# Turning v by VectorE in 32x32 blocks instead of by TensorE

## The chip, the core and the metric

The kernel runs on one core of a Trainium2 chip. The metric is the device time of one execution in microseconds (us), the median of several runs. The core's engines each work through a queue of their own in order: TensorE (PE in the profile; its weight loads are PEld), VectorE (DVE), ScalarE (ACT), GpSimd (POOL) and SyncE (SP), which here only issues DMAs. They wait for each other by semaphores. 16 DMA engines move data between device memory (HBM) and on-chip memory (SBUF); TensorE writes to PSUM, eight banks of 128 x 512 float32.

## The reference

Channel attention, and then a gated convolution over its output, for B = 4 batches of N = 6336 rows and C = 256 channels:

```python
qn = q / (np.linalg.norm(q, axis=1, keepdims=True) + 1e-06)
kn = k / (np.linalg.norm(k, axis=1, keepdims=True) + 1e-06)
s = kn.transpose(0, 2, 1) @ qn / tau
a = softmax(s)                                # 256 x 256 for each batch
x = v @ a
gate_pre[t] = sum(conv_w[j] * x[t - 4 + j] for j in range(5))   # x is 0 before row 0
gate = 1 / (1 + exp(-gate_pre))
out = (gate * (x @ w_val)) @ w_out
```

All inputs and the output are float32.

## The kernel before

**Two kinds of work.** A batch's scores s are summed in PSUM (s_ps) over 17 groups of rows of q and k; three rows per partition make a group (tile raw). A batch's output is made in 13 chunks of up to 508 rows of v, each with 4 rows of halo, so there are 52 steps (b, i). Batch 0's 17 groups come first, alone. From then on the remaining groups are spread over the steps up to the 36th ("steps with scores", until about 500 us); the last 16 steps have none ("steps without scores").

**Precision.** Most products are made of rounded parts: an operand is cast to a hi half (by ScalarE) and the rest is its lo half (one subtraction), and three products hi·hi, hi·lo, lo·hi are summed. So v has tiles v_hi and v_lo, the gated values g_hi and g_lo, and the scores' raw gets hi.

**A step.** `product` needs v with channels on partitions and rows along the free dimension, but v lies in memory by rows. `load_v` brings a chunk to v_raw by one DMA issued from SP (128 rows by 1 KB pieces, 512 KB). `transpose_v` turns it on TensorE, four 128x128 transposes for each half of the channels, to PSUM (t_ps, L359); ScalarE casts that to v_hi (L360) and VectorE subtracts to v_lo (L361). `conv` makes x_ps = v @ a by 6 products for each half h (L369); ScalarE scales the first tap to gate (L383) and VectorE adds the other four (L385). `sigmoid` (L391) is one instruction for both halves. `value` makes val_ps by 6 products with a @ w_val (L369), and VectorE multiplies it into gate (L398). `split_g` makes g_hi on ScalarE (L411) and g_lo on GpSimd (L412). `finish` makes 24 products with w_out (o_ps, L428), ScalarE copies them (L438) and issues the two stores (L443, L445).

**A group of scores.** ScalarE casts hi (L196) and squares (sq, L213), GpSimd makes the lo half (L197); VectorE and GpSimd add up the squares for the norms (L218); TensorE makes the products (L232). `softmax` of a batch is a chain of small instructions cut into pieces, which `tick` places between other work.

**What sets the order.** The program is written as a software pipeline: step n makes sigmoid(n), conv(n+1), value(n), split_g(n), transpose_v(n+2) and finish(n-1), and asks for load_v(n+3). A scheduler then orders each engine's queue by its own model of time, within what the program holds fast (`behind`, `high_priority`). Buffers tie queues together: three of v_raw, three of v_hi and v_lo, two banks of x_ps, and four banks shared by t_ps, val_ps and o_ps. A DMA also waits for the eighth DMA before it, whichever of SP and ScalarE issued that, since eight semaphores go round.

Of the kernel before, what the change touches and what calls it, by code (L numbers as in the profile page):

```python
# [29 lines left out]
def kernel(  # L30
# [301 lines left out]
    vraw, vt = {}, {}  # L332

    def load_v(b, i):

# [2 lines left out]
        j0 = 0
        if i == 0:
            nc.gpsimd.memset(t[0:HALO, 0, :], 0.0)  # L340
            nc.sync.dma_start(out=t[HALO:P, 0, :], in_=v[b, 0:P - HALO])
            j0 = 1
        full, rest = divmod(HALO + w, P)
        lo = t0 - HALO
        nc.sync.dma_start(out=t[:, j0:full, :], in_=v[b, lo + j0 * P:lo + full * P].rearrange("(j p) c -> p j c", p=P))
        if rest:
            nc.sync.dma_start(out=t[0:rest, full, :], in_=v[b, lo + full * P:t0 + w])
        vraw[b, i] = t

    def transpose_v(b, i, h):  # L350
        w = HALO + chunks[i][1]
        if h == 0:
            vt[b, i] = [v_p.tile([P, NH, HALO + WMAX], F32R, name=name) for name in ("v_hi", "v_lo")]
        th, tl = vt[b, i]
        src = vraw[b, i]
        tp = ps.tile([P, 512], F32, name="t_ps", tag="bank")
        for j in range(-(-w // P)):
            np_ = min(P, w - j * P)
            marks["PE"] = nc.tensor.transpose(tp[:, j * P:j * P + np_], src[0:np_, j, h * P:(h + 1) * P], ident[0:np_, 0:np_])  # L359
        nc.scalar.copy(th[:, h, 0:w], tp[:, 0:w])  # L360
        nc.vector.tensor_tensor(tl[:, h, 0:w], tp[:, 0:w], th[:, h, 0:w].bitcast(F32), ALU.subtract)  # L361
# [14 lines left out]
    def conv(b, i, h):  # L376
# [7 lines left out]
        for tap in range(1, K):  # L384
            nc.vector.scalar_tensor_tensor(gate[:, h, 0:w], x_ps[:, tap:tap + w], cw[:, h, tap:tap + 1],  # L385
                                           gate[:, h, 0:w], ALU.mult, ALU.add)

# [249 lines left out]
```

## Time and profile before

| | |
|---|---|
| median of 3 runs | 655.57 us (655.3 to 656.13) |
| profiled execution: span, first to last instruction | 653.5 us |
| granted TensorE clock, mean | 0.998 |
| read from HBM, written | 79.11 MB, 25.95 MB |

The profile is of one execution, whose span is 2.1 us (0.3%) under the median; the median also holds what lies around the instructions. An engine is busy while one of its instructions runs; issuing a DMA and waiting are not counted as busy. "x_ps<-v_hi,w" is an instruction that writes x_ps and reads v_hi and w. In a line of a group stand its count, its busy us in all, the mean ns of one, and after the last bar how long the engine had stood idle before these instructions and what ended that. Matmuls overlap, so their own lengths are longer than the distance from one to the next. The chain is the work that ended last, followed back from the last instruction through what released it.

### The profile page before, as it was taken

Reading aid. Unit: us, or ns where it says so; the run is one execution under the profiler, and the core shown is the slowest. Engines: PE = TensorE matmul, PEld = TensorE weight load, DVE = VectorE, ACT = ScalarE, POOL = GpSimd, SP = SyncE. Lnnn points to the kernel's source line nnn. Section 1 sums busy time; section 2 is a strip of 40 time slices with the busy share of each in tenths; the row PEclk is TensorE's granted clock in tenths of the full one; section 3 lists DMA queues with packets and bytes.
Section 4 is the critical chain, followed back from the end, with each engine's and each line's share of the span. In section 5 each row is a group of like instructions: output and inputs, shape, how many; then the busy total and the mean of one; then the engine's idle time right before and its main releaser. Section 6 shows DMA issues by size and latency. Waiting matters only on the chain.

```text
span 653.5 us, 10735 instructions
## 1 busy us (share of the span) xinstructions
PE 638.5 (98%) x4040; PEld 572.4 (88%) x4040; DVE 509.2 (78%) x831; ACT 466.8 (71%) x612; POOL 372.7 (57%) x181
## 2 busy tenths in 40 slices
PE   8899899999999999999999999999999899999996
PEld 7788699999989999998998999999989798888886
DVE  3694788887858787777877788887777879888884
ACT  4466978768688886777679887686877755655564
POOL 2591787949645786767855489496763122212221
PEclk9999999999999999999999999999999999999999
DMA  8999864646545564555645366453322343343213
GB/s 259 331 329 346 265 211 144 196 135 193 151 135 163 182 206 136 187 162 156 190 143 159 122 220 192 158 181 96 88 63 87 99 123 106 110 130 106 63 48 104
DMA packets 107876, 105.77 MB, mean 162 GB/s; under 512 B 5744, under 2 KB 107312, under 8 KB 107824
## 3 DMA queue, kind: packets, MB, share of 16 engines
q1 hardware_dynamic: 82048, 79.76, 39.6%
q10 hardware_dynamic: 25776, 25.32, 12.3%
q8 instruction: 32, 0.52, 0.3%
q14 instruction: 20, 0.16, 0.1%
HBM read 79.11 MB, written 25.95 MB: 161 GB/s over the span
## 4 chain that ended last, share of the span: by engine, by line
PE 87%; ACT 5%; SPq 3%; POOL 2%; issue 1%; DMA 1%; DVE 0%; ACTq 0%
PE o_ps L428 21%; PE x_ps L369 20%; PE val_ps L369 19%; PE s_ps L232 19%; PE t_ps L359 6%; SPq L75 2%; POOL hi L197 2%; DMA raw<-in_k_dram 1%; PE o_ps L318 1%; ACT hi L196 1%; ACT sq L213 1%; ACT L391 1%; ACT s L292 0%; SPq L125 0%; SPq L120 0%
## 5 line engine op out<-in xcount | busy, mean ns | idle before, releaser
L385 DVE SCALAR_TENSOR_TENSOR gate<-x_ps,wa,gate 128x508 f32<-128x508 f32 (+1 forms) x416 | 273.9, 716 | 15.8 <-ACT gate L383 14.9
L197 POOL TENSOR_TENSOR hi<-raw,hi 128x1536 fp32r<-128x1536 f32 (+2 forms) x51 | 166.1, 3259 | 103.2 <-ACT hi L196 103.2
L412 POOL TENSOR_TENSOR g_lo<-gate,g_hi 128x1016 fp32r<-128x1016 f32 (+1 forms) x50 | 117.5, 2351 | 125.9 <-ACT g_hi L411 125.8
L218 DVE TENSOR_TENSOR acc_ps<-acc_ps,sq 128x512 f32<-128x512 f32 (+1 forms) x124 | 86.5, 698 | 81.2 <-ACT sq L213 79.3
L369 PE MATMUL x_ps<-v_hi,w 128*128 128x512 f32 (+1 forms) x416 | 138.6, 392 | 0.5 <-DVE gate L385 0.3
L369 PE MATMUL val_ps<-v_hi,w 128*128 128x508 f32 (+1 forms) x416 | 134.1, 382 | 0.6 <-DVE w L323 0.5
L232 PE MATMUL s_ps<-hi 128*128 128x256 f32 (+1 forms) x846 | 119.6, 286 | 2.8 <-POOL hi L197 2.8
L232 PEld LDWEIGHTS s_ps<-hi 128*128 128x128 f32 (+1 forms) x846 | 109.6, 190 | 7.1 <-POOL hi L197 3.6
L428 PE MATMUL o_ps<-wo_hi,g_hi 128*128 128x256 f32 x400 | 112.9, 282 | 1.4 <-ACT at L313 1.4
L438 ACT COPY o_sb<-o_ps 128x512 f32<-128x512 f32 x99 | 58.2, 590 | 76.8 <-PE o_ps L428 76.6
L428 PE MATMUL o_ps<-wo_lo,g_hi 128*128 128x256 f32 x400 | 112.3, 281 | 0.0
L428 PE MATMUL o_ps<-wo_hi,g_lo 128*128 128x256 f32 x400 | 112.0, 280 | 0.0
L218 POOL TENSOR_TENSOR acc<-acc,sq 128x512 f32<-128x512 f32 x68 | 88.1, 1296 | 36.8 <-ACT sq L213 35.7
L213 ACT ACTIVATE sq<-raw 128x1536 f32<-128x1536 f32 (+3 forms) x69 | 95.9, 1393 | 15.8 <-DMA raw<-in_k_dram 10.4
L369 PEld LDWEIGHTS x_ps<-v_hi,w 128*128 128x128 f32 x416 | 77.4, 188 | 16.1 <-DVE gate L385 1.7
L369 PEld LDWEIGHTS val_ps<-v_hi,w 128*128 128x128 f32 x416 | 77.1, 188 | 14.4 <-DVE w L323 1.0
L383 ACT ACTIVATE gate<-x_ps,wa 128x508 f32<-128x508 f32 (+1 forms) x104 | 68.1, 669 | 18.8 <-PE x_ps L369 18.1
L398 DVE TENSOR_TENSOR gate<-val_ps,gate 128x508 f32<-128x508 f32 (+1 forms) x104 | 64.3, 657 | 21.7 <-ACT gate L391 20.0
L369 PE MATMUL x_ps<-v_lo,w 128*128 128x512 f32 (+1 forms) x208 | 79.6, 383 | 0.0
L369 PE MATMUL val_ps<-v_lo,w 128*128 128x508 f32 (+1 forms) x208 | 79.0, 380 | 0.0
L360 ACT CAST v_hi<-t_ps 128x512 fp32r<-128x512 f32 (+1 forms) x104 | 55.5, 570 | 32.9 <-PE t_ps L359 32.9
L428 PEld LDWEIGHTS o_ps<-wo_hi,g_hi 128*128 128x128 f32 x400 | 75.3, 188 | 2.3 <-ACT at L313 1.6
(80 smaller groups left out, 800.3 us busy)
## 6 DMA issues: line engine op xcount, KB each, us to landing
raw<-in_q_dram SPq DMA_DIRECT2D x64, 384.0 KB
raw<-in_k_dram SPq DMA_DIRECT2D x64, 384.0 KB
v_raw<-in_v_dram SPq DMA_DIRECT2D x44, 512.0 KB
out_dram<-o_sb ACTq DMA_DIRECT2D x47, 384.0 KB
out_dram<-o_sb ACTq DMA_DIRECT2D x47, 124.0 KB
v_raw<-in_v_dram SPq DMA_DIRECT2D x4, 384.0 KB
raw<-in_q_dram SPq DMA_DIRECT2D x4, 128.0 KB
raw<-in_k_dram SPq DMA_DIRECT2D x4, 128.0 KB
```

The costliest lines, as they stand in the source:

```text
L197: nc.gpsimd.tensor_tensor(hi[r, js, :, 1, :], raw[r, js, :, :], hi[r, js, :, 0, :].bitcast(F32), ALU.subtract)
L213: nc.scalar.activation(sq[0:np_, ja:jb], raw[0:np_, ja:jb], AF.Square)
L218: add = eng.tensor_tensor(st[key][0:np_], st[key][0:np_], sq[0:np_, j], ALU.add)
L232: marks["PE"] = nc.tensor.matmul(st["s"][:, h, :], lhs, rhs, start=False, stop=stop and h == NH - 1 and n_ == len(ops) - 1)
L360: nc.scalar.copy(th[:, h, 0:w], tp[:, 0:w])
L369: marks["PRODUCT"] = nc.tensor.matmul(ps, wt[:, which, ws, ch, hs], vs[:, ch, lo:hi_], start=n_ == 0, stop=n_ == 3 * NH - 1)
L383: nc.scalar.activation(gate[:, h, 0:w], x_ps[:, 0:w], AF.Copy, scale=cw[:, h, 0:1])
L385: nc.vector.scalar_tensor_tensor(gate[:, h, 0:w], x_ps[:, tap:tap + w], cw[:, h, tap:tap + 1], gate[:, h, 0:w], ALU.mult, ALU.add)
L398: nc.vector.tensor_tensor(gate[:, h, 0:w], val_ps[:, 0:w], gate[:, h, 0:w], ALU.mult)
L412: nc.gpsimd.tensor_tensor(gl[:, :, 0:w], gate[:, :, 0:w], gh[:, :, 0:w].bitcast(F32), ALU.subtract)
L428: nc.tensor.matmul(o_ps[:, u * C:(u + 1) * C], gs[:, h, off:off + P], ws[:, h, :], start=n_ == 0, stop=n_ == 3 * NH - 1)
L438: marks["ACT"] = nc.scalar.copy(o_sb[:, j:j + len(pair), :], o_ps[:, 0:len(pair) * C].rearrange("p (j c) -> p j c", c=C))
```

## The change

v is brought so that each 32x32 block lands in the quarter of the partitions where it belongs: v_raw now has dimensions [channel block j and row r in the block, half, block g of 32 rows, 32 channels], with eight DMAs for a chunk (four j, two h; sixteen for a batch's first chunk), each of 32 partitions and pieces of 128 bytes. Two VectorE instructions for each chunk (one for each half) then transpose all 32x32 blocks in place. ScalarE casts both halves in one instruction from SBUF. The lo halves are subtracted from SBUF: half 0 on VectorE and half 1 on GpSimd while groups of scores are left, both in one GpSimd instruction afterwards. Once all groups have been issued, the last of the five taps is no longer VectorE's: ScalarE scales it into a tile part, and GpSimd adds part to gate (all but the very last step). TensorE's transposes of v, and t_ps, are gone.

```diff
+    VW = -(-(HALO + WMAX) // Q) * Q                  # Q = 32
+    def span_v(i):
+        t0, w = chunks[i]
+        cols = -(-(HALO + w) // Q) * Q
+        base = min(t0 - HALO, N - cols)
+        return base, cols, t0 - HALO - base
     def load_v(b, i):
-        t = raw_p.tile([P, NT, C], F32, name="v_raw", bufs=3)
...
-        nc.sync.dma_start(out=t[:, j0:full, :], in_=v[b, lo + j0 * P:lo + full * P].rearrange("(j p) c -> p j c", p=P))
+        t = raw_p.tile([P, NH, VW // Q, Q], F32, name="v_raw", bufs=3)
+        for j in range(P // Q):
+            part = t[j * Q:(j + 1) * Q]
+            if base < 0:
+                nc.gpsimd.memset(part[0:-base, :, 0, :], 0.0)
+            for h in range(NH):
+                c0 = h * P + j * Q
...
+                nc.sync.dma_start(out=part[:, h, g0:g, :],
+                                  in_=v[b, base + g0 * Q:base + cols, c0:c0 + Q].rearrange("(g r) q -> r g q", r=Q))
-    def transpose_v(b, i, h):
...
-            marks["PE"] = nc.tensor.transpose(tp[:, j * P:j * P + np_], src[0:np_, j, h * P:(h + 1) * P], ident[0:np_, 0:np_])
-        nc.scalar.copy(th[:, h, 0:w], tp[:, 0:w])
-        nc.vector.tensor_tensor(tl[:, h, 0:w], tp[:, 0:w], th[:, h, 0:w].bitcast(F32), ALU.subtract)
+    def transpose_v(b, i):
...
+        for h in range(NH):
+            nc.vector.transpose(t[:, h, 0:g, :], t[:, h, 0:g, :])
+        marks["V"] = nc.scalar.copy(th[:, :, 0:g, :], t[:, :, 0:g, :])
+        for hs, eng in ((slice(0, 1), nc.vector), (slice(1, NH), nc.gpsimd)) if issued < len(all_groups) else ((slice(0, NH), nc.gpsimd),):
+            eng.tensor_tensor(tl[:, hs, 0:g, :], t[:, hs, 0:g, :], th[:, hs, 0:g, :].bitcast(F32), ALU.subtract)
     def conv(b, i, h):
...
-        for tap in range(1, K):
+        by_two = K - 1 if issued == len(all_groups) and all_steps.index((b, i)) < len(all_steps) - 1 else K
+        for tap in range(1, by_two):
             nc.vector.scalar_tensor_tensor(gate[:, h, 0:w], x_ps[:, tap:tap + w], cw[:, h, tap:tap + 1],
                                            gate[:, h, 0:w], ALU.mult, ALU.add)
+        for tap in range(by_two, K):
+            part = split_p.tile([P, WMAX], F32, name="part", tag="sq", bufs=2)[:, 0:w]
+            nc.scalar.activation(part, x_ps[:, tap:tap + w], AF.Copy, scale=cw[:, h, tap:tap + 1])
+            nc.gpsimd.tensor_tensor(gate[:, h, 0:w], gate[:, h, 0:w], part, ALU.add)
```

The scheduler orders the queues anew. Three places matter for what follows. The numbers behind names are buffers; in brackets stands what a row waits for (PE_, DVE_, Activation_, Pool_ are the engines, DMAHW0_ to DMAHW7_ the eight DMA semaphores).

SP in a step with scores, about the middle of the program, before: one load of v and the loads of q and k around it.

```order
L345 DMA v_raw_4119<-in_v_dram 128x4x256 [waits DMAHW5_49,PE_49]
L75 DMA raw_4139<-in_q_dram 128x3x256 [waits DMAHW6_49,Activation_49,Pool_49]
L75 DMA raw_4139<-in_k_dram 128x3x256 [waits DMAHW7_49]
L345 DMA v_raw_4258<-in_v_dram 128x4x256 [waits DMAHW3_49,DMAHW2_49,PE_49]
L75 DMA raw_4214<-in_q_dram 128x3x256 [waits DMAHW3_49,Activation_49,Pool_49]
L75 DMA raw_4214<-in_k_dram 128x3x256 [waits DMAHW4_49]
```

The same place after, where the gaps in the DMA numbers (1 and 3) are ScalarE's two stores:

```order
L76 DMA raw_4133<-in_k_dram 128x3x256 [waits DMAHW4_49]
L358 DMA v_raw_4243<-in_v_dram 32x16x32 [waits DMAHW5_49,DVE_49,Pool_49]
L358 DMA v_raw_4243<-in_v_dram 32x16x32 [waits DMAHW6_49]
L358 DMA v_raw_4243<-in_v_dram 32x16x32 [waits DMAHW7_49]
L358 DMA v_raw_4243<-in_v_dram 32x16x32 [waits DMAHW0_49]
L358 DMA v_raw_4243<-in_v_dram 32x16x32 [waits DMAHW2_49]
L358 DMA v_raw_4243<-in_v_dram 32x16x32 [waits DMAHW4_49]
L358 DMA v_raw_4243<-in_v_dram 32x16x32 [waits DMAHW5_49]
L358 DMA v_raw_4243<-in_v_dram 32x16x32 [waits DMAHW6_49]
L76 DMA raw_4208<-in_q_dram 128x3x256 [waits DMAHW7_49,Activation_49,Pool_49]
```

One row waiting for TensorE has become eight, the first of which waits for VectorE and GpSimd, and a store between them waits for the DMA eight before it, here a load of v or of q and k.

VectorE in the same step before, at the end of one chunk's work and the start of the next (gate_3901 and gate_4027 are the two chunks' gates):

```order
L218 TENSOR_TENSOR acc_ps_3575<-acc_ps_3575,sq_4019 128x512 [waits Activation_49]
L398 TENSOR_TENSOR gate_3901<-val_ps_4052,gate_3901 128x240 [waits PE_49,Activation_49]
L398 TENSOR_TENSOR gate_3901<-val_ps_4060,gate_3901 128x240 [waits DVE_49,PE_49]
L218 TENSOR_TENSOR acc_ps_3575<-acc_ps_3575,sq_4019 128x512 [waits DVE_49]
L361 TENSOR_TENSOR v_lo_4073<-t_ps_4074,v_hi_4072 128x512 [waits Activation_49]
L361 TENSOR_TENSOR v_lo_4073<-t_ps_4081,v_hi_4072 128x512 [waits Activation_49]
L385 SCALAR_TENSOR_TENSOR gate_4027<-x_ps_4028,wa_109,gate_4027 128x508 [waits Activation_49]
```

And after:

```order
L219 TENSOR_TENSOR acc_ps_3563<-acc_ps_3563,sq_4015 128x512 [waits Activation_49]
L414 TENSOR_TENSOR gate_3899<-val_ps_4048,gate_3899 128x240 [waits PE_49,Activation_49]
L414 TENSOR_TENSOR gate_3899<-val_ps_4056,gate_3899 128x240 [waits DVE_49,PE_49]
L219 TENSOR_TENSOR acc_ps_3563<-acc_ps_3563,sq_4015 128x512 [waits DVE_49]
L367 STREAM_TRANSPOSE v_raw_4243<-v_raw_4243 128x512 [waits DMAHW5_49,DMAHW7_49,DMAHW2_49,Pool_49]
L370 TENSOR_TENSOR v_lo_4220<-v_raw_3984,v_hi_4219 128x512 [waits Activation_49]
L367 STREAM_TRANSPOSE v_raw_4243<-v_raw_4243 128x512 [waits DMAHW6_49,DMAHW4_49,DMAHW0_49]
L397 SCALAR_TENSOR_TENSOR gate_4023<-x_ps_4024,wa_109,gate_4023 128x508 [waits Activation_49]
```

Two lo halves have become one lo half and two transposes, the transposes of a chunk a step ahead of its lo half and ahead of the next chunk's taps. The lo half v_lo_4069, whose v_raw buffer is the one that v_raw_4243 is loaded into, stands 15 rows above the first of these transposes; between them are two L414, eight taps and two sums.

ScalarE at batch 0's softmax before (s to exp, row sums to z, then a; `acc` and `sq` belong to batch 1's first groups):

```order
L209 ACTIVATE acc_455<-raw_356 128x512 [waits DMAHW7_49,DMAHW0_49]
L213 ACTIVATE sq_490<-raw_356 128x512 [waits Activation_49]
L292 ACTIVATE s_432,o_ps_465<-s_432,m_485 128x256 [waits DVE_49,PE_49]
L292 ACTIVATE s_432,o_ps_465<-s_432,m_485 128x256 [waits Activation_49]
L299 ACTIVATE a_507<-s_432,rz_505 128x256 [waits DVE_49]
```

And after:

```order
L210 ACTIVATE acc_477<-raw_373 128x512 [waits DMAHW6_49,DMAHW5_49]
L214 ACTIVATE sq_512<-raw_373 128x512 [waits Activation_49]
L368 CAST v_hi_603<-v_raw_379 128x1024 [waits DMAHW4_49,DMAHW3_49,DMAHW5_49,DMAHW2_49,DMAHW6_49,DMAHW1_49,DMAHW7_49,DMAHW0_49,DVE_49]
L293 ACTIVATE s_463,o_ps_487<-s_463,m_507 128x256 [waits DVE_49,PE_49]
L293 ACTIVATE s_463,o_ps_487<-s_463,m_507 128x256 [waits Activation_49]
L368 CAST v_hi_734<-v_raw_388 128x1024 [waits DMAHW4_49,DMAHW3_49,DMAHW5_49,DMAHW2_49,DMAHW6_49,DMAHW1_49,DMAHW7_49,DMAHW0_49,DVE_49]
L300 ACTIVATE a_529<-s_463,rz_527 128x256 [waits DVE_49]
```

The casts of the second and third chunk of v have come up into the softmax, ahead of the exponentials and of a, and wait for those chunks' loads and transposes.

More of the change, by code (lines that the diff above doesn't have):

```diff
@@ L23 @@
 VLEAD = 2
+Q = 32
 SIDE, LAST = 5, 15
@@ L332 @@
     vraw, vt = {}, {}
-    def load_v(b, i):
-        t0, w = chunks[i]
-        t = raw_p.tile([P, NT, C], F32, name="v_raw", bufs=3)
[L338 to L347, printed above, removed]
-        vraw[b, i] = t
@@ L350, in transpose_v @@
-    def transpose_v(b, i, h):
[L351 to L361, printed above, removed]
+    VW = -(-(HALO + WMAX) // Q) * Q
@@ new lines, in span_v @@
+    def span_v(i):
[3 more added lines that the diff above has]
+        return base, cols, t0 - HALO - base
+    def load_v(b, i):
+        base, cols, _ = span_v(i)
+        g = cols // Q
+        t = raw_p.tile([P, NH, VW // Q, Q], F32, name="v_raw", bufs=3)
[5 more added lines that the diff above has]
+                c0 = h * P + j * Q
+                g0 = 0
+                if base < 0:
+                    nc.sync.dma_start(out=part[-base:Q, h, 0, :], in_=v[b, 0:Q + base, c0:c0 + Q])
+                    g0 = 1
+                nc.sync.dma_start(out=part[:, h, g0:g, :],
+                                  in_=v[b, base + g0 * Q:base + cols, c0:c0 + Q].rearrange("(g r) q -> r g q", r=Q))
+        vraw[b, i] = t
@@ new lines, in transpose_v @@
+    def transpose_v(b, i):
+        g = span_v(i)[1] // Q
+        th, tl = vt[b, i] = [v_p.tile([P, NH, VW // Q, Q], F32R, name=name) for name in ("v_hi", "v_lo")]
+        t = vraw.pop((b, i))
+        for h in range(NH):
[3 more added lines that the diff above has]
+            eng.tensor_tensor(tl[:, hs, 0:g, :], t[:, hs, 0:g, :], th[:, hs, 0:g, :].bitcast(F32), ALU.subtract)
@@ L363, in product @@
     def product(ps, wt, which, b, i, h, lo, hi_):
-        th, tl = vt[b, i]
+        th, tl = (t.rearrange("p h g q -> p h (g q)") for t in vt[b, i])
+        at = span_v(i)[2]
+        lo, hi_ = at + lo, at + hi_
         hs = slice(h * P, (h + 1) * P)
@@ L525 @@
     tick()
-    with tc.high_priority(), behind("PE", "ACT"):
-        for h in range(NH):
-            transpose_v(*step(0), h)
+    with tc.high_priority(), behind("ACT"):
+        transpose_v(*step(0))
     with behind("PE", "ACT"):
@@ L550 @@
             nc.scalar.copy(wo_hi.rearrange("p h e -> p (h e)"), w_raw["out"][:, :, 1].bitcast(F32))
-    for h in range(NH):
-        transpose_v(*step(1), h)
+    transpose_v(*step(1))
     with behind("ACT"):
@@ L597 @@
         if new:
-            for h in range(NH):
-                transpose_v(*new, h)
+            transpose_v(*new)
         tick()
```

## The prediction

> **What bounds the kernel now.** I read the page's engine shares first, then its chain, then busy time by stage, then single groups, waits and DMA issues.
>
> ```profile
> PE 638.5 (98%) x4040; PEld 572.4 (88%) x4040; DVE 509.2 (78%) x831; ACT 466.8 (71%) x612; POOL 372.7 (57%) x181
> PE 87%; ACT 5%; SPq 3%; POOL 2%; issue 1%; DMA 1%; DVE 0%; ACTq 0%
> PE o_ps L428 21%; PE x_ps L369 20%; PE val_ps L369 19%; PE s_ps L232 19%; PE t_ps L359 6%; SPq L75 2%; POOL hi L197 2%; DMA raw<-in_k_dram 1%; PE o_ps L318 1%; ACT hi L196 1%; ACT sq L213 1%; ACT L391 1%; ACT s L292 0%; SPq L125 0%; SPq L120 0%
> ```
>
> TensorE carries 87% of the chain, and the transposes of v (t_ps, L359) are 6% of it: 0.062 x 653.5 = 40.5 us. That is the work the change takes off TensorE. The stages, 100 to 500 us (steps with scores) and 530 to 628.8 us (steps without); the columns are length, then busy us (and instructions) of PE, PEld, DVE, ACT and POOL, then clock, DMA share and GB/s:
>
> ```profile
> 100.00:500.00 400.00, 398.75 (x2649) 363.38 (x2648) 317.06 (x512) 310.53 (x393) 276.38 (x121) 1.00 0.51 156
> 530.00:628.80 98.80, 98.78 (x598) 87.37 (x597) 85.73 (x132) 57.21 (x87) 25.42 (x11) 1.00 0.33 103
> 403.14 1.02 PEld L359 LDWEIGHTS t_ps<-ident,v_raw 128*128 128x128 f32 x8
> 404.13 0.19 PEld L232 LDWEIGHTS s_ps<-hi 128*128 128x128 f32 x1
> ```
>
> TensorE is full in both stages. From the first weight load of a step's eight transposes to the next load are 404.13 - 403.14 = 0.99 us; 52 steps make at most 51 us. The other engines have room now: in the first stage VectorE is at 79%, ScalarE at 78%, GpSimd at 69%.
>
> **The change, part by part.** First the prices of single instructions (busy us, mean ns of one; or min/median/max ns):
>
> ```profile
> L361 DVE TENSOR_TENSOR v_lo<-t_ps,v_hi 128x512 fp32r<-128x512 f32 (+1 forms) x66 | 41.9, 662 | 0.0
> L360 ACT CAST v_hi<-t_ps 128x512 fp32r<-128x512 f32 (+1 forms) x66 | 35.3, 575 | 7.2 <-PE t_ps L359 7.2
> L303 DVE TENSOR_TENSOR w<-a,w x4: 681/682/693, 66.0 to 515.7; 128x512 fp32r<-128x512 f32 x4
> L151 DVE TENSOR_SCALAR w_raw<-w_raw 128x512 int32<-128x512 int32 (+1 forms) x3 | 3.7, 1248 | 0.0
> L409 POOL TENSOR_TENSOR g_lo<-gate,g_hi x2: 1314/1316/1317, 640.4 to 641.9; 128x508 fp32r<-128x508 f32 x2
> L412 POOL TENSOR_TENSOR g_lo<-gate,g_hi 128x1016 fp32r<-128x1016 f32 (+1 forms) x34 | 80.1, 2355 | 18.1 <-ACT g_hi L411 18.0
> L411 ACT CAST g_hi<-gate 128x1016 fp32r<-128x1016 f32 (+1 forms) x33 | 33.7, 1021 | 0.1
> L383 ACT ACTIVATE gate<-x_ps,wa 128x508 f32<-128x508 f32 (+1 forms) x66 | 43.5, 674 | 13.0 <-PE x_ps L369 12.7
> L385 DVE SCALAR_TENSOR_TENSOR gate<-x_ps,wa,gate 128x508 f32<-128x508 f32 x384 | 261.0, 738 | 15.2 <-ACT gate L383 14.3
> L443 ACTq DMA_DIRECT2D out_dram<-o_sb x50: 351/383/427, 99.6 to 642.7; - x50
> ```
>
> 66 lo halves in the first stage are 33 steps of 12.1 us. No row shows a block transpose of VectorE: 128x512 elements are nearest to L303 (0.68 us, SBUF to SBUF, same size), and L151 (1.25 us) is the upper end. I take 0.68.
>
> Steps with scores. TensorE loses 33 x 0.99 = 32.7 us, so its floor is 367.3. VectorE loses 41.9, gains 66 x 0.68 = 45 of transposes and 33 x 0.68 = 22.5 of lo halves: 342.7, 93% of the floor (at 1.25 us a transpose: 380, above it). GpSimd gains 33 x 1.32 = 43: 320, 87%. ScalarE has one cast of 1.02 in place of two of 0.575: 306, and with two store issues a step (66 x 0.38 = 25) 331, 90%. So everything fits, barely. What VectorE waits for now decides how much is given back:
>
> ```profile
> DVE acc_ps L218 <- ACT sq L213: 56.6, 41, 2.3
> DVE gate L385 <- ACT gate L383: 11.0, 19, 0.7
> DVE gate L398 <- ACT gate L391: 7.9, 6, 1.7
> ```
>
> That is 75 of its 83 idle us. If all waits shrink with the step, nothing is given back (367); if all stay, 342.7 + 83 = 425.7, slower than the 400 of now. A later VectorE waits less for ScalarE, but ScalarE in its order waits for VectorE's gate too, so I let half stay, 40 us: 382.7, of 32.7 us 15.4 are given back.
>
> Steps without scores (98.8 us, 10.8 steps of 9.15). TensorE 98.8 - 10.7 = 88.1. VectorE per step: minus two lo halves (1.32) and two taps (1.48), plus 1.36: 85.7 - 15.6 = 70. ScalarE: two taps of 0.67 more, the cast 0.13 less, stores 0.78: 57.2 + 13 + 8.4 = 78.7, 89%. GpSimd: one lo of 2.36 and two adds of 1.32: 25.4 + 54 = 79.4, 90%. The last tap now goes through ScalarE and GpSimd before the sigmoid, some 3 us more in the conv's line, which has about two steps between its product and its use. I give back 3 us (bounds 0 and all 10.7).
>
> Loads. One DMA of 512 KB becomes eight (v's first of each batch sixteen) of 128-byte pieces, 4096 instead of 508 per step.
>
> ```profile
> q1 hardware_dynamic: 82048, 79.76, 39.6%
> DMA packets 1194, 0.18 MB, mean 179 GB/s; under 512 B 1074, under 2 KB 1147, under 8 KB 1194
> q1 hardware_dynamic: 1194, 0.18, 118.5%
> 1.81 0.57 SPq L75 DMA_DIRECT2D raw<-in_k_dram  x1
> 4.21 0.60 ACT L209 ACTIVATE acc_ps<-raw 128x512 f32<-128x512 f32 x1 [1.97 <-DMA raw<-in_k_dram]
> ```
>
> A packet of about 1 KB costs 0.396 x 16 x 653.5 / 82048 = 50 ns. The second and third rows are the microsecond from 15 to 16, mostly conv_w's 8-byte pieces: 1.185 x 16 / 1194 = 16 ns. 128 bytes lie between; near the small end, 16 ns, a step's load takes 4096 x 16 / 16 = 4.1 us of the engines instead of 1.6: share (0.51 x 12.1 + 2.5) / 11.1 = 0.78. Hidden; at 50 ns it would be 12.9 us a step, longer than the step.
> The Trainium skill (DMA: Bandwidth & Descriptors, Specifications) speaks against such pieces: it gives 512 B as the least for line rate, with read-modify-write below. By it, at twice my price, the engines' share would be about 1.15 and a step some 12.8 us. No run here has shown 128-byte pieces.
>
> The start. The first v's are issued while batch 0's norms are finished (SP, start us, us):
>
> ```profile
> 43.81 0.33 SPq L341 DMA_DIRECT2D v_raw<-in_v_dram  x1
> 44.94 0.39 SPq L345 DMA_DIRECT2D v_raw<-in_v_dram  x1
> 49.45 1.27 SPq L345 DMA_DIRECT2D v_raw<-in_v_dram  x2
> 64.40 0.91 ACT L299 ACTIVATE a<-s,rz 128x256 f32<-128x256 f32 x2 [0.44 <-DVE rz L296]
> ```
>
> Four issues become 32: 28 x 0.42 = 12 us more on SP, with the next q and k behind them. The third v lands near 50.7 + 12 + 2.4 (landing, 4.21 - 1.81) = 65; two transposes and the cast later it is 67, and ScalarE now has that cast ahead of batch 0's a, which started at 64.40. I take 4 us (bounds -1, if SP's waits absorb it, and 13).
>
> Sum: 653.5 - 40.5 + 4 + 15.4 + 3 = 635.4 us of span. The median before, 655.57, is 2.1 above the span; I add it: 637.5 us. Likely 622 to 650 if this case holds.
>
> **Rivals.**
> 1. All of it fits: nothing given back, 655.6 - 40.5 = 615 (604 if all 51 us count). For it: 87% of VectorE beside a full TensorE in the second stage is already there. Against: four engines near 90% in queues that wait for each other.
> 2. VectorE's lo half stands behind GpSimd. It reads two SBUF operands, which so far only L303 and the tail do.
>
> ```profile
> 404.96 1.06 ACT L411 CAST g_hi<-gate 128x1016 fp32r<-128x1016 f32 x1
> 406.10 2.41 POOL L412 TENSOR_TENSOR g_lo<-gate,g_hi 128x1016 fp32r<-128x1016 f32 x1 [0.47 <-ACT g_hi L411]
> 515.17 1.06 ACT L411 CAST g_hi<-gate 128x1016 fp32r<-128x1016 f32 x1
> 515.68 0.68 DVE L303 TENSOR_TENSOR w<-a,w 128x512 fp32r<-128x512 f32 x1
> 516.37 2.42 POOL L412 TENSOR_TENSOR g_lo<-gate,g_hi 128x1016 fp32r<-128x1016 f32 x1 [10.90 <-ACT g_hi L411]
> L197 POOL TENSOR_TENSOR hi<-raw,hi 128x1536 fp32r<-128x1536 f32 (+2 forms) x45 | 149.4, 3322 | 102.2 <-ACT hi L196 102.2
> L218 POOL TENSOR_TENSOR acc<-acc,sq 128x512 f32<-128x512 f32 x39 | 50.8, 1303 | 0.0
> ```
>
> GpSimd started 0.08 us after its cast at 406.10, but 0.14 at 516.37, 0.01 after L303's end: a hint of exclusion, no more. If they exclude each other, a lo half meets on average (45 x 3.32² + 34 x 2.36² + 72 x 1.31²) / 2 / 367 = 1.1 us of a running GpSimd instruction: 36 us over the stage, VectorE 379, with half of the other waits 399. The first stage then gains nothing, and the rest (40.5 - 32.7 - 7) 0.8: 655, between 645 and 668.
> This is a rule of the Trainium skill (SBUF — State Buffer, Who interferes with whom): a VectorE instruction with two SBUF inputs and a GpSimd one that reads SBUF fully block each other, by order of issue. The trace's hint agrees, without proof.
> 3. Slower: the reload loop. A v_raw buffer was free when TensorE had transposed it; now it is free after both lo halves, then come eight issues (3.4 us) and the landing (2.4), and VectorE's next transposes stand in its queue 6 to 8 us behind its lo half (two L398, eight taps, one or two sums). GpSimd's half, behind hi and a sum, can end 4.6 us later: 10.4 in all, then VectorE stands 2.5 us a step with all taps behind it: 342.7 + 33 x 2.5 = 425, about 680 us. It decides from 0.5 us a step beyond my 40 us of waits. For it: ScalarE's stores can wait for these loads as well, since a DMA waits for the eighth before it. Against: GpSimd has idle time before most of its waits.
> 4. The small pieces cost more. A step with scores has 0.51 x 12.1 - 1.6 = 4.6 us of other transfers, so from (11.1 - 4.6) x 16 / 4096 = 26 ns the DMA engines bound it, and from 29 ns it is slower than now; at 50 ns a step takes 17.5 us, some 830 us in all.
>
> **Chances.** Forecast 0.45; rival 1 0.15; rival 2 0.18, a third of it each faster, same, slower; rival 3 0.18; rival 4 0.04. A measurement here tells 0.2% from no change, 1.3 us. Faster: 0.45 + 0.15 + 0.07 = 0.67, plus a little of rival 3's mild form, 0.70; same 0.06; slower 0.24. The range from 612 to 668 leaves out rival 1's full form, most of rival 3 and rival 4, under 0.2.
>
> **What would show it.** Block transposes near 0.68 us; TensorE's span of a step with scores 11.1 to 11.7 us instead of 12.1, without scores 8.2 to 8.5. Wrong if VectorE's transposes wait for DMA v_raw by over 0.5 us a step (rival 3), if VectorE's lo halves are much longer than 0.68 or GpSimd's start at VectorE's ends (rival 2), if the DMA share is at 0.9 between 100 and 450 us (rival 4), or if a starts over 10 us later than 64.4.

## The result and the profile after

The changed kernel takes 732.5 us (median of 4 runs, 722.75 to 736.79) against 655.43 before: a ratio of 1.109 (95% interval 1.103 to 1.115). Medians in this text are of all runs, but some runs fell in a slower state of the chip, and every ratio and every difference between two versions leaves these out, which makes 726.7 us of this kernel and, further down, 712.6 of taps_on_vector and 644.2 of late_second_load. The change makes the kernel slower by 11%, where 637.5 us had been forecast and 668 was the upper end of the range. The profiled execution has a span of 728.9 us, 75.4 more than that of before.

Engine shares, DMA share in 40 slices of the span (in tenths) and chain on the page of the changed kernel:

```profile
PE 630.0 (86%) x3640; PEld 549.6 (75%) x3640; DVE 554.3 (76%) x835; ACT 484.3 (66%) x592; POOL 502.7 (69%) x277
DMA  8977997465667486755474477564334454534112
PE 19%; SPq 17%; DMA 16%; DVE 16%; issue 11%; POOL 10%; ACT 10%; ACTq 0%; POOLq 0%; DVEq 0%
SPq L358 11%; DMA v_raw<-in_v_dram 9%; PE o_ps L444 7%; DVE gate L397 6%; PE x_ps L380 5%; PE val_ps L380 4%; DVE v_lo L370 4%; SPq L76 4%; DMA out_dram<-o_sb 3%; POOL v_lo L370 3%; POOL acc L219 2%; POOL g_lo L428 2%; DMA raw<-in_q_dram 2%; DVE gate L414 2%; DMA raw<-in_k_dram 2%
```

The 400 transposes are gone from TensorE, and so is its hold on the time: it carries 19% of the chain instead of 87%. No engine took its place. Each is idle for 14 to 34% of the span, and the chain goes round through all of them, with the issue of v's loads (SPq L358, 11%), their landing (9%) and v_lo (4 and 3%) as its largest new pieces. That is a pipeline bound by its waits. The two stages that the prediction used (length, then busy us and instructions of PE, PEld, DVE, ACT, POOL, then clock, DMA share, GB/s):

```profile
100.00:500.00 400.00, 348.77 (x2155) 309.21 (x2154) 343.18 (x495) 277.67 (x325) 297.83 (x147) 0.97 0.63 155
530.00:628.80 98.80, 87.75 (x514) 76.47 (x512) 70.06 (x115) 72.66 (x103) 69.48 (x42) 0.98 0.46 97
```

VectorE is as busy as forecast (342.7), but that is chance: it gets through fewer steps, and its lo halves take longer. The waits of the changed kernel that answer to the prediction's list (us in total, times, longest), and the two operations of v on VectorE and GpSimd (ns min/median/max):

```profile
DVE v_raw L367 <- DMA v_raw<-in_v_dram: 46.3, 25, 5.8
DVE acc_ps L219 <- ACT sq L214: 41.9, 32, 5.7
DVE gate L397 <- ACT gate L394: 40.0, 23, 5.2
SPq L358 <- POOL v_lo L370: 97.3, 29, 12.1
SPq L358 <- DVE v_lo L370: 63.5, 22, 10.6
L367 DVE STREAM_TRANSPOSE v_raw<-v_raw x104: 401/698/717, 55.2 to 670.4; 128x512 f32<-128x512 f32 x96, 128x256 f32<-128x256 f32 x8
L370 DVE TENSOR_TENSOR v_lo<-v_raw,v_hi x36: 408/1564/9748, 58.2 to 521.8; 128x512 fp32r<-128x512 f32 x34, 128x256 fp32r<-128x256 f32 x2
L370 DVE TENSOR_TENSOR v_lo<-v_raw,v_hi 128x512 fp32r<-128x512 f32 (+1 forms) x36 | 66.6, 1849 | 1.8 <-ACT v_hi L368 1.7
```

Two things stand out. The block transpose costs about what was assumed, 0.70 us for 0.68. The lo half does not: 66.6 us for 36 of them, where 34 at 0.68 and 2 at 0.41 make 24. And VectorE waits 46.3 us for v's loads, which it never did before. The two SPq rows are SP's waits before it may issue a load of v into a used buffer: GpSimd's lo half freed the buffer last in 29 cases, VectorE's in 22.

Where the time went, by the starts of sigmoids (52, one for each step; the 4th to the 36th are the steps with scores after the start):

| start of sigmoid, us | 1st | 4th | 36th | 52nd | 4th to 36th | 36th to 52nd |
|---|---|---|---|---|---|---|
| before | 81.6 | 115.0 | 499.4 | 643.6 | 384.4 | 144.2 |
| changed | 93.8 | 145.9 | 562.2 | 717.9 | 416.3 | 155.7 |

12.2 us are lost up to the first sigmoid, 18.7 to the fourth, 31.9 in the 32 steps to the 36th, 11.5 in the last 16, and 1.1 behind: 75.4. The forecast had been +4 for the start, -17.3 for the steps with scores and -7.7 for those without.

### The profile page after: what moved, and what is told of

It is laid out like the page before. It is cut to its first block, busy times and chain, and to the rows that moved or that the text cites. A ratio compares the mean times of both kernels' runs of the same rounds, so it can differ in the third digit from the quotient of the medians.

```text
span 728.9 us, 10770 instructions
## 1 busy us (share of the span) xinstructions
PE 630.0 (86%) x3640; PEld 549.6 (75%) x3640; DVE 554.3 (76%) x835; ACT 484.3 (66%) x592; POOL 502.7 (69%) x277
## 4 chain that ended last, share of the span: by engine, by line
PE 19%; SPq 17%; DMA 16%; DVE 16%; issue 11%; POOL 10%; ACT 10%; ACTq 0%; POOLq 0%; DVEq 0%
SPq L358 11%; DMA v_raw<-in_v_dram 9%; PE o_ps L444 7%; DVE gate L397 6%; PE x_ps L380 5%; PE val_ps L380 4%; DVE v_lo L370 4%; SPq L76 4%; DMA out_dram<-o_sb 3%; POOL v_lo L370 3%; POOL acc L219 2%; POOL g_lo L428 2%; DMA raw<-in_q_dram 2%; DVE gate L414 2%; DMA raw<-in_k_dram 2%
## 5 line engine op out<-in xcount | busy, mean ns | idle before, releaser
L397 DVE SCALAR_TENSOR_TENSOR gate<-x_ps,wa,gate 128x508 f32<-128x508 f32 (+1 forms) x384 | 261.3, 713 | 42.7 <-ACT gate L394 40.0
L380 PE MATMUL x_ps<-v_hi,w 128*128 128x512 f32 (+1 forms) x416 | 147.1, 405 | 38.0 <-DVE gate L397 26.2
L380 PEld LDWEIGHTS x_ps<-v_hi,w 128*128 128x128 f32 x416 | 81.3, 197 | 58.9 <-issue 17.1
L444 PE MATMUL o_ps<-wo_hi,g_lo 128*128 128x256 f32 x400 | 109.1, 288 | 11.8 <-POOL g_lo L428 11.6
L219 POOL TENSOR_TENSOR acc<-acc,sq 128x512 f32<-128x512 f32 x68 | 92.3, 1357 | 24.6 <-ACT sq L214 23.3
L367 DVE STREAM_TRANSPOSE v_raw<-v_raw 128x512 f32<-128x512 f32 (+1 forms) x104 | 68.4, 674 | 53.4 <-DMA v_raw<-in_v_dram 46.3
L370 POOL TENSOR_TENSOR v_lo<-v_raw,v_hi 128x512 fp32r<-128x512 f32 (+2 forms) x52 | 86.7, 1668 | 30.3 <-ACT v_hi L368 21.9
L407 ACT ACTIVATE gate<-gate 128x1016 f32<-128x1016 f32 (+1 forms) x52 | 52.9, 1018 | 58.5 <-DVE gate L397 53.7
L444 PEld LDWEIGHTS o_ps<-wo_hi,g_lo 128*128 128x128 f32 x400 | 74.4, 192 | 15.5 <-POOL g_lo L428 13.8
L380 PE MATMUL x_ps<-v_lo,w 128*128 128x512 f32 (+1 forms) x208 | 82.9, 398 | 0.0
```

Of the source, the lines that this page charges most:

```text
L219: add = eng.tensor_tensor(st[key][0:np_], st[key][0:np_], sq[0:np_, j], ALU.add)
L367: nc.vector.transpose(t[:, h, 0:g, :], t[:, h, 0:g, :])
L370: eng.tensor_tensor(tl[:, hs, 0:g, :], t[:, hs, 0:g, :], th[:, hs, 0:g, :].bitcast(F32), ALU.subtract)
L380: marks["PRODUCT"] = nc.tensor.matmul(ps, wt[:, which, ws, ch, hs], vs[:, ch, lo:hi_], start=n_ == 0, stop=n_ == 3 * NH - 1)
L444: nc.tensor.matmul(o_ps[:, u * C:(u + 1) * C], gs[:, h, off:off + P], ws[:, h, :], start=n_ == 0, stop=n_ == 3 * NH - 1)
```

## The experiments

**Two suspects.** Theory A: the reload loop (rival 3). Theory B: VectorE and GpSimd exclude each other (rival 2). In the timeline of the changed kernel (start us, us) the plainest place for B is this:

```profile
104.09 3.52 POOL L198 TENSOR_TENSOR hi<-raw,hi 128x1536 fp32r<-128x1536 f32 x1
107.57 1.28 POOL L219 TENSOR_TENSOR acc<-acc,sq 128x512 f32<-128x512 f32 x1
108.81 1.26 POOL L370 TENSOR_TENSOR v_lo<-v_raw,v_hi 128x512 fp32r<-128x512 f32 x1
110.03 3.41 POOL L198 TENSOR_TENSOR hi<-raw,hi 128x1536 fp32r<-128x1536 f32 x1
113.40 1.26 POOL L219 TENSOR_TENSOR acc<-acc,sq 128x512 f32<-128x512 f32 x1
105.46 9.75 DVE L370 TENSOR_TENSOR v_lo<-v_raw,v_hi 128x512 fp32r<-128x512 f32 x1
```

VectorE's lo half stood through five GpSimd instructions that ran without a gap, and ended 0.55 us after the last (113.40 + 1.26 = 114.66; 105.46 + 9.75 = 115.21). It is the extreme one, but not the only one: 29 of the 36 lo halves take over 0.8 us, and 28 of these ended 0.55 us after the end of a GpSimd instruction (the other one, 0.28 us after). The case for A is the chain, around 320 us (pieces of 0.02 to 0.04 us marked issue are left out):

```profile
318.37 1.72 POOL v_lo L370
320.10 0.33 SPq L358
...
323.14 0.49 SPq L358
323.67 4.76 DMA v_raw<-in_v_dram
...
328.55 0.71 DVE v_raw L367
329.26 0.63 DVE gate L397
329.88 2.38 DVE v_lo L370
```

GpSimd's lo half frees a buffer at 320.1, eight issues and the landing take until 328.4, and the next lo half stands in VectorE's queue behind the transposes that waited for them.

**five_buffers, half_by_psum, both, one_load.** The edits:

```diff
# five_buffers
-        t = raw_p.tile([P, NH, VW // Q, Q], F32, name="v_raw", bufs=3)
+        t = raw_p.tile([P, NH, VW // Q, Q], F32, name="v_raw", bufs=5)
# half_by_psum, in steps with scores
+            tp = ps.tile([P, 512], F32, name="t_ps", tag="bank")...
+            nc.vector.transpose(tp, t[:, 0, 0:g, :])
+            nc.vector.transpose(t[:, 1, 0:g, :], t[:, 1, 0:g, :])
+            nc.scalar.copy(th[:, 0, 0:g, :], tp)
+            nc.scalar.copy(th[:, 1, 0:g, :], t[:, 1, 0:g, :])
+            nc.vector.tensor_tensor(tl[:, 0, 0:g, :], tp, th[:, 0, ...], ALU.subtract)
+            nc.gpsimd.tensor_tensor(tl[:, 1, 0:g, :], t[:, 1, ...], th[:, 1, ...], ALU.subtract)
# one_load, in place of the loops over j and h
...
+        nc.sync.dma_start(out=out_t, in_=v[b, b0:b0 + cols].rearrange("(j p) c -> p j c", p=P))
```

> The changed kernel (732.5 us) with five v_raw buffers instead of three, nothing else. Theory A, the reload loop: VectorE's 46.3 us of waits for DMA v_raw are the price of a buffer that comes free only after both lo halves and is then refilled by eight issues (4.1 us) and a landing (4.8 us). With two more buffers these waits fall under 10 us and the time to 690 us or below. Theory B, exclusion: VectorE's lo halves hold for running GpSimd instructions (36 of them took 66.6 us, 43 more than at 0.68 us each), and that is what delays everything; then the time stays at 720 to 735 and the lo halves stay at a median near 1.5 us. If both act, 690 to 715 with the long lo halves still there.

Measured: 735.3 us, ratio 1.124 (1.119 to 1.128). Nothing came back (it is 8.6 us slower), and VectorE still waited for v's loads:

```profile
DVE v_raw L367 <- DMA v_raw<-in_v_dram: 52.4, 24, 5.8
```

Its lo halves stayed long (median 1.38 us), as B said, but they took 50.7 us in all instead of 66.6, and the time did not follow. So the length of the lo halves alone does not set the time either.

> The changed kernel with three v_raw buffers, but in steps with scores half 0 of v is transposed from v_raw into a PSUM bank; ScalarE casts it from there (two casts of 512 instead of one of 1024) and VectorE's lo half reads PSUM and SBUF instead of two SBUF operands. GpSimd's half stays. Theory B: VectorE's lo halves fall from a median of 1.56 to 0.68 us, 43 us of VectorE's time come back, and the time falls to 690 to 700. Theory A: the buffer still waits for GpSimd's half, the DMA waits of VectorE stay at 40 us or more and the time at 715 to 735.

Measured: 693.1 us, 1.058 (1.055 to 1.061): 33.6 us come back. The lo half in this kernel:

```profile
L372 DVE TENSOR_TENSOR v_lo<-t_ps,v_hi x36: 412/681/691, 56.7 to 497.5; 128x512 fp32r<-128x512 f32 x34, 128x256 fp32r<-128x256 f32 x2
```

Not one of the 36 is longer than 0.69 us: with one operand in PSUM the exclusion is gone, and B is shown as a cause. The 33.6 us are the price of the edit as a whole, since it also lets go of half 0's buffer before the lo half and casts in two instructions. The waits for v's loads did not shrink by it, though: 57.1 us in all, against 46.3.

> Both edits: half 0 through PSUM and five v_raw buffers. If A and B are two separate prices they add: 732 less 43 less some 40, 640 to 655, near the kernel before, with the later start (12 us at the first sigmoid, 31 us by the fourth step) and the steps without scores (11 us more than before) still paid. If they are one loop (a late lo half frees the buffer late) the sum is smaller: 670 to 690, no better than the better one alone.

Measured: 706.1 us, 1.079 (1.076 to 1.083), worse than half 0 through PSUM alone and outside both ranges: more buffers cost 13 us here.

> The changed kernel with each chunk of v brought by one DMA of 1 KB pieces as before, in place of eight (sixteen) of 128-byte pieces. The layout that the transposes need is left out, so v's blocks are in the wrong places. It shows what issuing and landing the many small loads costs. Theory A: 3.7 us of issue and some 2 us of landing leave a loop that runs every step, and the start gets back its 12 us at the first sigmoid: 680 to 700. Theory B alone: only the start comes back, 710 to 722, and VectorE's lo halves stay long.

Measured: 698.6 us, 1.066 (1.064 to 1.068). This is in A's range: 28.1 us are the price of eight small loads for a large one. Of the 32.5 us between the two profiled executions, 21.5 lie up to the fourth sigmoid (124.4 instead of 145.9). The lo halves stay long (50 us for 36), and VectorE's waits for v's loads stay at 44.6 us, so the loop that A means still runs. So the loads count, mostly at the start, and not through the number of buffers. This run changes the number of issues and the size of the pieces together. Both can count there, as the DMA share shows (third number from the right is the clock, then the share and GB/s); the changed kernel, 80 to 120 us:

```profile
80.00:100.00 20.00, 18.28 (x99) 15.26 (x98) 15.14 (x20) 17.45 (x18) 14.98 (x7) 1.00 0.91 202
100.00:120.00 20.00, 8.33 (x50) 7.16 (x49) 20.00 (x18) 6.55 (x7) 14.66 (x8) 0.82 0.93 229
```

The DMA engines are almost full here, where one_load has shares of 0.58 and 0.60 and the kernel before 0.61 and 0.58. Which of the two it is was not separated.

**Why buffers did not help.** The order of VectorE's queue went along with them. The lo halves and transposes in VectorE's order, with the rows between them left out; the buffer that v_raw_2355 is loaded into, with three, is that of v_raw_1954, and with five v_raw_2492 takes that of v_raw_1777:

```
three buffers:
L370 TENSOR_TENSOR v_lo_2196<-v_raw_1954,v_hi_2195 128x512
L367 STREAM_TRANSPOSE v_raw_2355<-v_raw_2355 128x512
L367 STREAM_TRANSPOSE v_raw_2355<-v_raw_2355 128x512
L370 TENSOR_TENSOR v_lo_2318<-v_raw_2104,v_hi_2317 128x512
five buffers:
L370 TENSOR_TENSOR v_lo_2065<-v_raw_1777,v_hi_2064 128x256
L367 STREAM_TRANSPOSE v_raw_2492<-v_raw_2492 128x512
L367 STREAM_TRANSPOSE v_raw_2492<-v_raw_2492 128x512
L370 TENSOR_TENSOR v_lo_2196<-v_raw_1954,v_hi_2195 128x512
```

Either way, between one lo half and the next stand the transposes of the very chunk that the first lo half let in: lo half, issues, landing, transposes, next lo half. In these two orders that is so for 22 and 23 of the 36 lo halves; for the others one to three lo halves stand between. The scheduler places transposes as early as a buffer allows, so the loop is closed again whatever the number. What opens it is a rule for the order: a chunk's transposes behind the lo half of the chunk before it, so that two more lo halves stand between the one that frees its buffer and its transposes.

**held, held_psum, taps_on_vector, taps_alone.**

```diff
# held (and the same line around the transposes of half_by_psum: held_psum)
+            with behind("LO") if "LO" in marks else nullcontext():
                 nc.vector.transpose(t[:, h, 0:g, :], t[:, h, 0:g, :])
# taps_on_vector; taps_alone is the kernel before with the opposite edit
-        by_two = K - 1 if issued == len(all_groups) and all_steps.index((b, i)) < len(all_steps) - 1 else K
+        by_two = K
```

> The changed kernel (732.5 us, three buffers) with one rule more for the order: the two transposes of a chunk are issued after the lo half of the chunk before it, not ahead of it. Five buffers gave 735.3 us, because VectorE's order went along: the transposes of a chunk stood again just ahead of the lo half that frees the buffer which is loaded next. Theory A in this form (the reload loop is closed by the order of VectorE's queue, not by the number of buffers): VectorE's waits for DMA v_raw fall from 46 us to under 15 and the time to 690 to 705. Theory B (exclusion alone): lo halves stay at a median near 1.5 us and the time at 715 to 735.

Measured: 720.4 us, 1.099 (1.097 to 1.102). The waits went nearly as A said, the time did not: it fell by 6.3 us and is in B's range.

```profile
DVE v_raw L368 <- DMA v_raw<-in_v_dram: 15.5, 7, 5.3
```

Likely, while the exclusion holds, opening the loop mostly lets VectorE run sooner into the next GpSimd instruction: its 36 lo halves take 69.5 us, one of them 10.9.

> The held order together with half 0 through PSUM (693 us by itself). If reload loop and exclusion are separate prices: 655 to 670, what is left over the kernel before being the later start (12 us at the first sigmoid, some 10 more by the fourth step) and the steps without scores (11 us). If they are one and the same delay: 685 to 695, no better than half 0 through PSUM alone.

Measured: 663.6 us, 1.015 (1.010 to 1.019), inside the range for two prices, but they do not add. Alone, half 0 through PSUM gave 33.6 us and the held order 6.3, 39.9 in all; together they give 63.1. Each is worth more once the other is there: the held order 29.5 us after PSUM (693.1 to 663.6), PSUM 56.8 after the held order (720.4 to 663.6). The steps with scores of this kernel, 100 to 480 us, have TensorE nearly full again:

```profile
100.00:480.00 380.00, 373.93 (x2407) 338.07 (x2406) 333.71 (x549) 311.62 (x393) 325.10 (x166) 1.00 0.70 169
```

From the 4th to the 36th sigmoid it takes 495.5 - 127.7 = 367.8 us, 16.6 less than before.

> The changed kernel with the last tap left on VectorE in steps without scores as well; everything else as changed. In the changed kernel the 16 last sigmoids take 155.7 us instead of 144.2. If the way of the last tap over ScalarE and GpSimd is what costs there (POOL and PE wait 15.5 and 17 us for part): 718 to 725. If it is GpSimd's whole lo half at the end of its queue and the reload behind it: no change, 728 to 738.

Measured: 716.9 us, 1.092 (1.085 to 1.099), just under the first range. The last 16 sigmoids take 149.2 us instead of 155.7, 6.5 less. The profiled execution is 19.1 us shorter in all, though, and 11.4 of them lie before the 36th sigmoid, 8.3 even before the second, where the two kernels' queues are the same row for row. So the time of this run does not price the tap. The place shown above, in this execution:

```profile
102.89 3.49 POOL L198 TENSOR_TENSOR hi<-raw,hi 128x1536 fp32r<-128x1536 f32 x1
106.34 1.74 POOL L219 TENSOR_TENSOR acc<-acc,sq 128x512 f32<-128x512 f32 x1
104.29 2.65 DVE L370 TENSOR_TENSOR v_lo<-v_raw,v_hi 128x512 fp32r<-128x512 f32 x1
```

Here VectorE got in between hi and acc (which was held for 0.45 us in turn, 1.74 instead of 1.28) and stood for 2 us, not 9. Who gets in is settled by small differences in time, which is a likely cause of the scatter of the changed kernel's runs (14 us; before, 1.2).

> The kernel before with only this one part of the change: in steps without scores the last tap by ScalarE and GpSimd. TensorE is full there (98.78 of 98.8 us), so nothing can be won; 655 to 656 if it is hidden, as GpSimd is idle at 26% there, 660 to 668 if the longer line from x_ps to the sigmoid is late by 0.3 to 0.8 us in each of the 16 steps.

Measured: 660.0 us, 1.008 (1.006 to 1.010). In the kernel before, the split tap alone costs 5 us, though VectorE's work falls: TensorE is still full in 530 to 628.8 us. Of the 4.8 us between the two spans 2.4 lie between the 36th and the 52nd sigmoid (146.6 instead of 144.2) and 1.8 behind the last.

**held_psum_taps, late_second_load.** Both taken together with the start:

```diff
# late_second_load, beside held order, half 0 through PSUM and taps on VectorE
-                for nv in range(1, VLEAD + 1):
-                    load_v(*step(nv))
+                load_v(*step(1))
...
+    load_v(*step(VLEAD))
     tick()
     for h in range(NH):
         conv(*step(0), h)
# transposes of batch 0's chunks: behind("LO", "W"), W being the lo half of w in softmax
# halo rows of both halves in one DMA
```

> Held order, half 0 through PSUM (663.6 us together), and the last tap left on VectorE in all steps. The last 16 sigmoids took 156 us there against 144 before; with the tap back on VectorE they took 149 in the otherwise unchanged version. If the split tap costs the same here: 655 to 658, the same as before within 0.5%, made of a gain of 17 us in steps with scores and a loss of some 12 at the start and 5 at the end. If the steps without scores are bound by GpSimd's whole lo half and the reload: 661 to 665.

Measured: 658.8 us, 1.005 (1.004 to 1.007), 4.8 less than held_psum and just outside the first range. The last 16 sigmoids still take 154.4 us (156.3 in held_psum), not 149: here the tap was not what held them.

> The same, and the start mended: the halo rows of a first chunk come in four DMAs instead of eight, the third chunk is loaded after batch 1's first groups instead of ahead of their q and k, and the transposes of the second and third chunk are issued behind batch 0's w, not inside its softmax. If the start is late (12 us at the first sigmoid) because of SP's 32 issues and of VectorE standing at the second chunk's transposes (5.8 us of wait for its load ahead of the scaling of s), it comes back by 5 to 10 us: 645 to 652, faster than before. If the start is late because the loads' transfers take the DMA engines from q and k, nothing changes: 654 to 660.

Measured: 645.9 us, 0.983 (0.981 to 0.986): the first version that is faster than before. The reason given for the start is seen on VectorE in the changed kernel (the last row is TensorE's):

```profile
60.45 0.22 DVE L277 TENSOR_SCALAR nk<-o_ps,rtau 128x2 f32<-128x2 f32 x1
66.47 1.46 DVE L367 STREAM_TRANSPOSE v_raw<-v_raw 128x512 f32<-128x512 f32 x2 [5.80 <-DMA v_raw<-in_v_dram]
67.85 0.67 DVE L219 TENSOR_TENSOR acc_ps<-acc_ps,sq 128x512 f32<-128x512 f32 x1
68.42 0.85 DVE L288 SCALAR_TENSOR_TENSOR s<-s,nk,o_ps 128x256 f32<-128x256 f32 x2
69.19 1.69 DVE L370 TENSOR_TENSOR v_lo<-v_raw,v_hi 128x512 fp32r<-128x512 f32 x1
64.73 0.76 PE L285 MATMUL o_ps<-diag,ones 128*128 128x128 f32 x4
```

The second chunk's transposes stood in the middle of batch 0's softmax and waited 5.8 us for a load that nothing needed yet, with the scaling of s behind them. The scaling also needs TensorE's product of L285, which ended at 65.5, so at most 2.9 us of its delay (68.42 less 65.5) are the transposes'. Three things were changed at once here, and ScalarE's casts moved back as well, so their shares are open. The first sigmoid starts at 86.7 instead of 94.7. That lead of 8.0 us is 5.7 at the 36th sigmoid. Of the 14.2 us between the two profiled executions another 8.8 lie in the last 16 sigmoids (145.6 instead of 154.4), on which this edit was not meant to act, and that was not traced.

**probe_sbuf, probe_psum.** The exclusion by itself, in the kernel before:

```diff
         nc.vector.tensor_tensor(tl[:, h, 0:w], tp[:, 0:w], th[:, h, 0:w].bitcast(F32), ALU.subtract)
+        if h == 0 and issued < len(all_groups):
+            nc.vector.tensor_tensor(scrap[:, 0:w], tl[:, h, 0:w].bitcast(F32), th[:, h, 0:w].bitcast(F32), ALU.subtract)
# probe_psum: tp[:, 0:w] in place of tl[:, h, 0:w]
```

> The kernel before (655 us, v turned by TensorE), with one VectorE subtraction of 128x512 more in each of the 36 steps that make v while scores are left: v_lo less v_hi of half 0, both in SBUF, into a scrap tile that nobody reads. It prices the exclusion apart from loads, buffers and order. Exclusion: these 36 instructions take a median of 1.2 us or more instead of 0.68, each ending with or after a GpSimd instruction, and the time rises to 660 to 675. No exclusion: 0.68 us each, 24 us of VectorE's 83 idle us in 100 to 500 us, and the time stays within 0.5% of 655.

> The same, but the added subtraction reads t_ps in PSUM and v_hi in SBUF. Exclusion holds for two SBUF operands only: 0.68 us each and 655 to 658. If any added VectorE work of this size delays the step, the time is that of the run with two SBUF operands.

Measured: 665.4 us, 1.015 (1.013 to 1.017), and 658.7 us, 1.005 (1.004 to 1.007). The added instruction in each:

```profile
L364 DVE TENSOR_TENSOR scrap<-v_lo,v_hi x36: 402/952/3653, 57.2 to 490.0; 128x512 f32<-128x512 f32 x34, 128x244 f32<-128x244 f32 x2
L364 DVE TENSOR_TENSOR scrap<-t_ps,v_hi x36: 400/679/684, 55.5 to 480.8; 128x512 f32<-128x512 f32 x34, 128x244 f32<-128x244 f32 x2
```

One operand's place lengthens the instruction: 24 of the 36 take over 0.8 us, and each of these ended 0.55 us after a GpSimd instruction. The median, 0.95 us, is under the expected 1.2. In time it makes 6.7 us, but not 36 small losses: in the profiled executions probe_sbuf is already 8.8 us behind probe_psum at the third sigmoid, after two instructions of 3.0 and 3.7 us at the start, and 7.0 at the last. In the steps with scores after that the longer instructions cost nothing, since VectorE still had slack.

**held_five, psum_all_steps.** What was left open were the last 16 steps.

> The best version so far (645.9 us: held order, half 0 by PSUM, taps on VectorE, third load later) with five v_raw buffers. With the order held, more buffers are real slack. If the steps without scores are bound by the reload loop through GpSimd's lo half, the last 16 sigmoids fall from 145.6 to some 136 to 140 us and the time to 637 to 641. If not: 644 to 648.

Measured: 673.0 us, 1.027 (1.026 to 1.029), 28.8 us worse than with three buffers, and the last 16 sigmoids took 152.6 us: missed on both counts. One place is plain, on ScalarE (a second store between the last two rows is left out):

```profile
108.84 1.49 ACT L214 ACTIVATE sq<-raw 128x1536 f32<-128x1536 f32 x1
118.68 0.42 ACTq L470 DMA_DIRECT2D out_dram<-o_sb  x1
119.92 1.05 ACT L418 ACTIVATE gate<-gate 128x1016 f32<-128x1016 f32 x1 [9.59 <-DMA v_raw<-in_v_dram]
```

A store waits for the DMA eight before it, here a load of v that had been asked for early; ScalarE and the sigmoid behind the store stood for 9.6 us. That explains 10 of the 28.8 us at most; the rest was not traced.

> The best version so far with half 0 through PSUM, and the lo halves shared by VectorE and GpSimd, in the steps without scores too. GpSimd's lo half is 1.3 us there instead of 2.4 and ends earlier, VectorE has 0.68 us a step more. If the loop through GpSimd binds those steps: 638 to 643. If VectorE does (it is busy 84.6 of 98.8 us there and would have 7.3 more): 645 to 652.

Measured: 643.3 us, 0.980 (0.977 to 0.982), at the edge of the first case; its interval overlaps that of late_second_load, so which of the two is faster is open. Its last 16 sigmoids took 149.9 us, against 145.6 without the edit, so if it gained, it was not where the edit acts. Why the steps without scores stay at 145 to 150 us, with TensorE busy for 90 of 98.8, is not settled.

## Why the prediction was wrong, point by point

- **TensorE's gain (-40.5) and the give-back in steps with scores (+15.4): near as a sum, but only in a kernel without the two rivals, and in part by luck.** 32.7 - 15.4 = 17.3 us were forecast for that stage; held_psum has 16.6 between the 4th and 36th sigmoid, with VectorE, ScalarE and GpSimd at 88, 82 and 86% of 380 us. But late_second_load has 20.9 there and psum_all_steps 26.8, and half of the waits was a choice between two ends, not a reading. The kernel as changed has +31.9. (The stages' gains, 32.7 and 10.7, also make 43.4, not the 40.5 of the sum: one came from weight loads, the other from the chain.)
- **The lo half at 0.68 us: the step that failed first.** Its price was taken from L303, which at 515.68 ran while GpSimd had nothing to do, though the very next row showed GpSimd starting 0.01 us after its end. Rival 2 had the size right: 1.1 us more per lo half, against (66.6 - 24) / 36 = 1.18 measured. It had 0.18 of the chance, and its effect on the time was put at 17 us (655 for 637.5); taking it away gave 33.6, or 56.8 with the held order.
- **The reload loop (rival 3) was real too.** The mark for it, over 0.5 us a step of VectorE's waits for DMA v_raw, was passed (46.3 us). Its price was seen as that of three buffers and a line of 10.4 us from the lo half to the landing; the runs showed that VectorE's order closes it, and that opening it gives 6.3 us while the exclusion holds and 29.5 without it.
- **Rivals weighed as alternatives: the larger fault.** Each was worked out alone, 655 and 680. Both sat on the lo halves: VectorE's stands behind GpSimd, and it and GpSimd's are what free the buffer (22 and 29 of the waits). A late end there is a late load, late transposes and late taps. The 728.9 us came from the two together with the start and the last 16 steps, which no case of the prediction held.
- **The start (+4, bounds -1 and 13).** a started at 73.7, 9.3 later than before, inside the bounds, but the first sigmoid 12.2 later and the fourth 30.9. The prediction blamed ScalarE's cast. In the trace ScalarE waits at the first two casts (5.0 and 4.0 us), VectorE at the transposes inside the softmax (5.8), and the loads of v fill the DMA engines; which weighs most is open. Part of the 30.9 is the exclusion: half_by_psum has the fourth sigmoid at 131.9, 14.0 earlier. With the exclusion and the loop away, it is 12.7 late.
- **Steps without scores (-10.7 + 3).** They lost 11.5. The split tap was costed at a delay hidden by two steps, and the worst case was that the stage gains nothing; in the kernel before, it alone costs 5 us. What else holds these steps is open.
- **Small pieces: the price per packet held, and rival 4 did not come in the steps with scores.** The first queue of the changed kernel and of one_load:

```profile
q1 hardware_dynamic: 267424, 79.83, 46.9%
q1 hardware_dynamic: 82080, 79.83, 36.9%
```

The second is 0.369 x 16 x 696.4 / 82080 = 50 ns a packet. The difference between the two is (0.469 x 728.9 - 0.369 x 696.4) x 16 = 1358 us of engine time; with 25,600 pieces of 1 KB in one_load at 50 ns (1283 us), the 210,944 packets in their place took 12.5 ns each, under the 16 assumed. (The prediction's price at which the DMA engines bound a step, 26 ns, is 25 by its own sum.) The DMA share in 100 to 500 us is 0.63, and 0.70 to 0.71 in held_psum and late_second_load from 100 to 480, so the DMA engines did not bound these steps as a whole. From 80 to 120 us, at 0.91 and 0.93, they may have, which the prediction's average over a step does not see. Per byte 128-byte pieces are about twice as dear as 1 KB ones (128 / 12.5 = 10 bytes a ns against 20), which is the direction of the minimum of 512 B that the Trainium skill gives (DMA: Bandwidth & Descriptors, Specifications). The cost of the small loads is likely their number on one issuing queue, and at the start the full DMA engines; no run separates the two.

The edits, one on the other, give 726.7, 693.1 (half 0 through PSUM), 663.6 (held order), 658.8 (tap on VectorE) and 644.2 us (start, though more than half of that step lies in the last 16 sigmoids). That is within 6.7 us of the forecast, but of another kernel than the one forecast, so it does not bear the forecast out.

## What to carry to other kernels

Before work is moved to VectorE or GpSimd, look at where each operand lies: a VectorE instruction with two SBUF inputs beside a busy GpSimd must be priced at what GpSimd is running, not at its own length, and one operand in PSUM takes the price away. What it costs in time depends on the slack: in the kernel before, where VectorE had room, 36 such instructions cost 6.7 us, all of it at the start, and in the changed kernel taking them away gave 33.6. When two delays sit on the same instruction, price them together: here the two repairs gave 39.9 us one by one and 63.1 together. And where a scheduler places a prefetch as early as a buffer allows, more buffers are not slack; look in the queue at what stands between the release and the next use, and hold the early instruction back.
